# Decay attention and a softplus feed-forward on one core: the middle blocks of the feed-forward at 384 tokens instead of 256, with three output banks and x in four places of 128 tokens

## The chip, the cores and the metric

The kernel runs on one core of a Trainium2 chip. A core has a matrix engine (TensorE, PE), which reads from the on-chip memory SBUF and writes to eight banks of PSUM; a vector engine (VectorE, DVE), a scalar engine (ScalarE, ACT) and a slower general engine (GpSimd, POOL); and a sync engine (SyncE, SP) that issues the DMAs here. Each engine works through its own list of instructions in order, and they wait for each other by semaphores. The metric is the time of one execution on the device, in microseconds (us), less being better. The kernel before takes 1237.31 us, the median of three runs (1235.45 to 1237.55).

## What is computed

Eight batches of 576 tokens, eight heads of 64. First attention with a decay: each score gets the difference of two running sums of log f. Then its output, seen as 4608 tokens of 512 numbers, goes through a feed-forward with 2048 hidden columns and a softplus.

```python
scores = scale * np.matmul(q, k.transpose(0, 1, 3, 2))
log_f = np.log(np.clip(f, 0.0001, 1.0))
cum = np.cumsum(log_f, axis=-1)
decay = cum[:, :, :, None] - cum[:, :, None, :]
scores = np.where(causal, -1000000000.0, scores + decay)
...
x = np.ascontiguousarray(attn_out.transpose(0, 2, 1, 3)).reshape(B * S, H * D)
h = x @ w_in
g = np.maximum(h, 0.0) + np.log1p(np.exp(-np.abs(h)))
return (g @ w_out).astype(np.float32)
```

Inputs are fp32, the two weights 64-bit floats.

## The kernel before

**Numbers in two parts.** Most products are made of rounded numbers (type fp32r) in a high and a low part: an up product takes x high by w high, x low by w high, x high by w low. That is 12 matmuls for each group of 128 hidden columns (`fc`, 16 of them) and a block of tokens: four chunks of 512/128 by three. Down products take the same three pairings of g and w_out, three matmuls of 512 columns for each `fc` and tile of 128 tokens. The high part of w_in (`wih`) and both parts of w_out (`woh`, `wol`) stay in SBUF; the low part of w_in is stored to HBM once (`wil_d`) and loaded again for every block, 512 KB for each two `fc` (`wl`).

**Weights.** The 64-bit weights come in 32 pieces (`load_f64`). A piece is built as fp32 from the two halves of each number by a `scale` (ACT), `clip` (POOL or DVE), `shift`, `low` and `sign` (DVE). Afterwards `split_w_in` and `split_w_out` part it into high and low.

**Attention.** It is cut into 68 jobs: 4 for two heads of the first 256 tokens of batch 0, 8 for the rest of batch 0 by head, then 56, one for each head of batches 1 to 7. Jobs 0 to 11 use plain fp32 matmuls (L723, L853); from job 12 on they are in two parts. A job's score tiles (`s`, L725 and L726) are read by DVE for the row minimum (L730) and by ACT for the exponential (L750); the weights are scaled, turned by PE (`b`, L805), copied by ACT or DVE in two parts (L205, L820), multiplied with v (`o`, L859), and put into the batch's x (`x32`, L877 and L886). Every `s`, `b` and `o` takes one PSUM bank with the tag `att`, of which there are four.

**Feed-forward.** `BLOCKS` cuts the 4608 tokens into 14 blocks of 256 and 2 of 512. Block 0 is plain fp32 (L996, L1100). For the others `split_x` makes the two parts of x, xh and xl, in an array of two halves of 256 tokens: blocks of 256 take turns in the halves (tags x0 and x1), a block of 512 takes both. `up_part` issues six up matmuls (L1016) into a bank `h` (two of them), `gate` computes the softplus of 512 columns of a bank (ACT L1052, L1055, L1058; DVE L1066; high and low parts, L205 and L1074), and `down_part` multiplies with w_out (L1107) into one bank for each tile of 128 tokens: two banks `acc` for a block of 256; a block of 512 takes two more of `att`. The down products of a bank come two banks (`LAG`) after its up products.

**What sets the order.** The program is first written down as operations (`Plan.add`) with what they come after and which buffers (`takes`, `give`) they need. `Plan.run` then puts them in order with an estimate of each one's time: of the next 600 that are free to go it takes the one that could start first. Where it sees PE idle ahead of the first feed-forward output it puts filler matmuls (L1219). A block may be written down once its batch's attention is done (`ready_at`: by job 11, 19, 27 and so on). Feed-forward work is laid between the pieces of the jobs by a share:

```python
until = min((at for at in ready_at if at >= n), default=n)
share = sum(c for c, _ in ffn) / (until - n + 1 + DELAY) / max(1, len(units))
```

So what is at hand is spread over the jobs until the next blocks may begin, and `DELAY` jobs more.

Of the kernel before, what the change touches and what calls it, by code (L numbers as in the profile page):

```python
# [26 lines left out]
DELAY = 6  # L27
# [140 lines left out]
def on_dve(n, fast=False, port=False, bias=0.0):  # L168
    return On("DVE", 0.071 + n / (1920 if fast else 960), bias, fast or port)
# [18 lines left out]
def copies(n):  # L188

    return [on_act(n), on_dve(n, True, bias=COPY_BIAS)]  # L190
# [18 lines left out]
def tile_decay_attention_softplus_ffn(  # L209
# [36 lines left out]
    BUFS = dict(T=2, att=4, h=2, acc=2, xs=1, fe=4, ph=3, pl=3, ph64=2, pl64=2, gh=LAG + 1, gl=LAG + 1, xh=1, xl=1,  # L246
                x32=2, wl=2, vhl=3, vraw=2, raw=1)
    plan = Plan(BUFS | dict(T0=4, stat=4, p=2, x0=1, x1=1, x2=1))
# [147 lines left out]
    def load_f64(src, new, name, takes=()):  # L396
# [27 lines left out]

        def shift(e):
            x = box["x"] = new().bitcast(U32)
            e.tensor_scalar(x, box["t"].bitcast(U32), 3, None, ALU.logical_shift_left)
# [5 lines left out]
        def sign(e):  # L433
            x, h = box["x"], box["t"].bitcast(U32)
            e.scalar_tensor_tensor(x, h, 0x80000000, x, ALU.bitwise_and, ALU.bitwise_or)

# [493 lines left out]
    def ffn_block(i):  # L930

        t0, nt = BLOCKS[i]
        wide = nt > TB
        ntile = nt // P
        nk = 512 // nt
        tags = ("acc", "acc", "att", "att")[:ntile]
        st = {"ups": [], "downs": []}
        plain = i == 0
        half = i % 2
        xtags = ("x0", "x1", "x2") if wide or i == 1 else (f"x{half}",)  # L940

        def split_x():
            if plain:
                st["split"] = [d for a, _, d in wrote[0] if a < TB]
                return
            ready, at = [], t0
            while at < t0 + nt:
                b, o = at // S, at - t0
                lo = at - b * S
                w = min(t0 + nt - at, S - lo, TB - o % TB)  # L950

                def part(x, o=o, w=w):
                    return x_now[x][:, o // TB if wide else half, :, o % TB : o % TB + w]

                def hi_part(e, b=b, lo=lo, w=w, o=o, part=part):
                    if o == 0 and (wide or i == 1):
                        for x in ("xh", "xl"):
                            x_now[x] = buf(x, [P, 2, NCC, TB], f"{x}{i}", F32R)
                    copy(e, part("xh"), x_of[b][:, :, lo : lo + w])

                def lo_part(e, b=b, lo=lo, w=w, part=part):
                    hi = part("xh").bitcast(F32)
                    e.tensor_sub(part("xl"), x_of[b][:, :, lo : lo + w], hi)

                need = [d for a, z, d in wrote[b] if a < lo + w and z > lo]
                h_ = add(
                    copies(NCC * w), hi_part, after=need + ready[:1], takes=() if o else xtags,
                )
                if i == 1 and not o:
                    give("x0", [h_])  # L970
                    give("x2", [h_])
                l_ = add(subs(NCC * w), lo_part, after=[h_])
                ready += [h_, l_]
                splits.setdefault(b, []).append(l_)
                if lo + w == S:
                    give("x32", splits[b])
                at += w
            st["split"] = ready

        def up_part(u, k, part):  # L980
# [8 lines left out]
            def mm(e):  # L989
                if first:  # L990
                    st["h", u] = bank("h", f"h{i}_{u}")
                    st["x", "h"], st["x", "l"] = x_now.get("xh"), x_now.get("xl")
# [8 lines left out]
                if wide:  # L1001
                    o = o.rearrange("p (a t) -> p a t", a=2)
                wl, todo = st["wl", fp], []

                def x(t, cc):
                    t = st["x", t]
                    return t[:, :, cc] if wide else t[:, half, cc]
# [24 lines left out]
            if plain:  # L1032
                for p in pieces:
                    w_in_read.setdefault(p, []).append(op)
                if fc == NFC - 1:
                    splits.setdefault(0, []).append(op)
            elif fc % 2 == 1 and part == 1:
                give("wl", [op])
                if fc == NFC - 1:
                    for x in xtags if i > 1 else ("x1",):  # L1040
                        give(x, [op])

        def gate(fp):
# [3 lines left out]
            def view(a):  # L1047
                return a.rearrange("p (k t) -> p k t", k=nk)
# [132 lines left out]
    for i, (t0, nt) in enumerate(BLOCKS):  # L1181
# [40 lines left out]
    old = nothing  # L1222
    for n in range(len(jobs) + 1):
# [33 lines left out]
        share = sum(c for c, _ in ffn) / (until - n + 1 + DELAY) / max(1, len(units))  # L1257
# [53 lines left out]
```

## Time and profile before

| what | before |
|---|---|
| median of three runs | 1237.31 us (1235.45 to 1237.55) |
| the profiled execution: its own time, its span | 1236.16 us, 1234.4 us |
| mean granted clock of TensorE | 0.994 of full |
| instructions | 21512 |
| moved by DMA | 143.33 MB, mean 116 GB/s |

The profile is of one execution. Its page gives each engine's busy time, groups of equal instructions with their mean time and the idle time ahead of them, and the chain of work that ended last, followed back from the end. In the chain PE has 74% of the span and DVE 13%; L1016 has 28% and L1107 27%. Between two cuts, a table of windows gives each engine's busy time. Times of attention's jobs are those of their first score matmul in the trace: job 12 at 137.1 us, job 24 at 277.2, job 67 at 984.0; the last attention matmul is at 1007.8, and from there PE has the feed-forward alone.

### The profile page before, as it was taken

How to read it: one execution, taken by the hardware profiler on the slowest of the kernel's cores; microseconds unless marked ns; L12 is line 12 of the kernel's file. 1: busy time of each engine (PE TensorE's matmuls, PEld its weight loads, DVE VectorE, ACT ScalarE, POOL GpSimd, SP SyncE). 2: the span in 40 equal slices, each digit the busy share in tenths (PEclk: the TensorE clock that was granted, in tenths of full speed). 3: DMA queues.
4: the chain of work that ended last, by engine and by line, in shares of the span. 5: the costliest groups of instructions: out<-in, count | busy, mean ns of one | idle time of the engine just before them, and what ended most of it. 6: DMA issues, size and time to landing. Idle time of an engine off the chain costs nothing.

```text
span 1234.4 us, 21512 instructions
## 1 busy us (share of the span) xinstructions
PE 1214.8 (98%) x7648; PEld 1066.9 (86%) x7648; DVE 869.1 (70%) x2175; ACT 870.4 (71%) x2069; POOL 156.5 (13%) x130
## 2 busy tenths in 40 slices
PE   8899999999999999999999999999999999999998
PEld 6666678898999999999999999999988999888887
DVE  7898999998887887676777677777778852323322
ACT  5577788978887777676776778677878754444543
POOL 4742011110110111010111001100010100000000
PEclk9899999999999999999999999999999999999999
DMA  7864534443354334343433444334434223211210
GB/s 223 262 176 133 153 92 145 128 123 119 110 152 116 121 109 117 112 130 111 118 119 95 135 118 136 99 114 118 136 102 134 73 69 103 68 52 51 86 52 35
DMA packets 53355, 143.33 MB, mean 116 GB/s; under 512 B 6656, under 2 KB 21016, under 8 KB 53248
## 3 DMA queue, kind: packets, MB, share of 16 engines
q1 hardware_dynamic: 53248, 141.95, 38.5%
q8 instruction: 61, 1.00, 0.4%
q14 instruction: 46, 0.38, 0.1%
HBM read 127.85 MB, written 14.07 MB: 115 GB/s over the span
## 4 chain that ended last, share of the span: by engine, by line
PE 74%; DVE 13%; ACT 5%; DMA 3%; issue 2%; POOL 1%; SPq 1%; DVEq 0%; ACTq 0%; POOLq 0%
PE h L1016 28%; PE acc L1107 27%; PE o L859 6%; PE b L805 6%; PE s L725 3%; PE s L726 3%; DVE s L730 2%; ACT p L773 2%; ACT p L750 1%; DMA raw<-in_qkT 1%; DVE pl L820 1%; PE acc L1100 1%; POOL ti L423 1%; DVE T L681 1%; DMA xl_st<-in_w_out 1%
## 5 line engine op out<-in xcount | busy, mean ns | idle before, releaser
L1016 PE MATMUL h<-xh,wih 128*128 128x256 f32 (+1 forms) x960 | 277.2, 312 | 0.8 <-DVE gl L1074 0.8
L1016 PE MATMUL h<-xl,wih 128*128 128x256 f32 (+1 forms) x960 | 262.9, 297 | 0.0
L1107 PE MATMUL acc<-woh_dt_float32r,gh 128*128 128x512 f32 x544 | 221.8, 408 | 0.0
L750 ACT ACTIVATE p<-s,negm 128x288 f32<-128x288 f32 (+7 forms) x384 | 183.0, 479 | 50.2 <-DVE negm L730 47.7
L1107 PE MATMUL acc<-woh_dt_float32r,gl 128*128 128x512 f32 x544 | 213.4, 392 | 0.0
L1107 PE MATMUL acc<-wol_dt_float32r,gh 128*128 128x512 f32 x544 | 213.0, 391 | 0.0
L1066 DVE SCALAR_TENSOR_TENSOR h<-h,e 128x512 f32<-128x512 f32 x136 | 95.2, 701 | 152.4 <-ACT e L1058 151.9
L775 POOL TENSOR_SCALAR p<-p,rsum 128x448 f32<-128x448 f32 (+4 forms) x77 | 97.7, 1275 | 754.7 <-DVE rsum L764 476.3
L1016 PEld LDWEIGHTS h<-xh,wih 128*128 128x128 f32 x960 | 182.7, 190 | 7.3 <-DVE gl L1074 1.2
L1016 PEld LDWEIGHTS h<-xl,wih 128*128 128x128 f32 x960 | 183.0, 191 | 5.8
L730 DVE CUSTOM_DVE_ANT_0 s<-s,cmask 128x288 f32<-128x288 f32 (+5 forms) x320 | 137.2, 438 | 54.7 <-PE s L726 46.6
L1016 PE MATMUL h<-xh,wl 128*128 128x256 f32 (+1 forms) x960 | 167.9, 297 | 0.0
L1052 ACT ACTIVATE e<-h 128x512 f32<-128x512 f32 x144 | 85.7, 595 | 111.5 <-PE h L1016 109.6
L820 DVE TENSOR_TENSOR pl<-b,ph 128x512 fp32r<-128x512 f32 (+1 forms) x224 | 125.9, 569 | 41.7 <-ACT ph L205 39.5
L805 PE MATMUL b<-ident,p 128*128 128x128 f32 x960 | 147.0, 277 | 7.9 <-ACT p L773 4.2
L1016 PEld LDWEIGHTS h<-xh,wl 128*128 128x128 f32 x960 | 138.4, 190 | 4.9
L805 PEld LDWEIGHTS b<-ident,p 128*128 128x128 f32 x960 | 112.7, 141 | 27.6 <-ACT p L773 6.5
L773 ACT ACTIVATE p<-p,rsum 128x576 f32<-128x576 f32 (+7 forms) x221 | 105.8, 542 | 28.8 <-DVE rsum L764 28.6
L1107 PEld LDWEIGHTS acc<-woh_dt_float32r,gl 128*128 128x128 f32 x544 | 102.2, 188 | 22.7
L1074 DVE TENSOR_TENSOR gl<-h,gh 128x512 fp32r<-128x512 f32 x136 | 93.6, 688 | 34.8 <-ACT gh L205 33.4
L1107 PEld LDWEIGHTS acc<-wol_dt_float32r,gh 128*128 128x128 f32 x544 | 102.9, 189 | 15.0
L1107 PEld LDWEIGHTS acc<-woh_dt_float32r,gh 128*128 128x128 f32 x544 | 102.8, 189 | 15.0
(107 smaller groups left out, 2142.8 us busy)
## 6 DMA issues: line engine op xcount, KB each, us to landing
wl<-wil_d SPq DMA_DIRECT2D x120, 512.0 KB
raw<-in_qkT SPq DMA_DIRECT2D x112, 288.0 KB
vr<-in_vR SPq DMA_DIRECT2D x64, 160.0 KB
out<-ob SPq DMA_DIRECT2D x36, 256.0 KB
sto<-in_w_out SPq DMA_DIRECT2D x11, 512.0 KB
sti<-in_w_in SPq DMA_DIRECT2D x9, 512.0 KB
wil_d<-wil SPq DMA_DIRECT2D x16, 256.0 KB
xh_st<-in_w_in SPq DMA_DIRECT2D x5, 512.0 KB
```

Of the source, the lines that this page charges most:

```text
L730: e.tensor_tensor_reduce(out=box["o"], in0=box["o"], in1=cmask[0:n_q, right - w : right], scale=-0.125, scalar=m0 if i else 3.0e38, op0=AL ...
L750: e.activation(o, box["o"], AF.Exp, bias=m1, scale=-1.0, accum_out=acc)
L773: e.activation(a, a, AF.Copy, scale=f_)
L775: e.tensor_scalar(a, a, f_, None, ALU.mult)
L805: e.transpose(box["ps"][:, at : at + P], pt[pi][:, c : c + P], ident)
L820: e.tensor_sub(box["l"], box["ps"][:, pad : pad + w], box["h"].bitcast(F32))
L859: e.matmul(box["ps"][:, a - g0 : z - g0], st["vhl"][:, vc, :], pbox[x][:, o : o + z - a], start=i == 0 and m == 0, stop=i == len(todo) - 1 ...
L1016: e.matmul(o, l, r, start=m == 0, stop=m == 11)
L1052: e.activation(box["e"], view(st["h", fp]), AF.Abs)
L1066: e.scalar_tensor_tensor(h, h, 0.0, box["e"], ALU.max, ALU.add)
L1074: e.tensor_sub(box["l"], box["t"], box["h"].bitcast(F32))
L1107: e.matmul(st["acc"][tt], l, r[fc], start=fc == 0 and m == 0, stop=fc == NFC - 1 and m == 2,)
```

## The change

Tokens 512 to 3583 are cut into eight blocks of 384 in place of twelve of 256. The array of x has four places of 128 tokens (tags s0 to s3): a block of 384 takes places 0 to 2 or 1 to 3 in turn, so that one place of the next block is free before the block ahead of it is done with the other three; `split_x` works by place, the free one first. A block of 384 has one `fc` in a bank `h` (`nk` is 1), and its gate covers 384 columns. There are three banks `acc` and three `att`; a block of 512 takes three `acc` and one `att`. In `load_f64` the sign is taken as the product of the clipped number and 0.0, on POOL or DVE, into a buffer `gh`, and put in by the shift. `DELAY` is 1, and the share is held below one that spreads what is at hand and what is still to come over all jobs left.

```diff
-DELAY = 6
+DELAY = 1
...
-    TB, WIDE = 256, 512
-    BLOCKS = [(t, TB) for t in range(0, NT - 2 * WIDE, TB)] + [(NT - 2 * WIDE, WIDE), (NT - WIDE, WIDE)]
+    TB = 256
+    BLOCKS = [(0, TB, 0), (TB, TB, 0)]
+    BLOCKS += [(t, 384, t // 384 % 2) for t in range(512, NT - 1024, 384)]
+    BLOCKS += [(NT - 1024, 512, 0), (NT - 512, 512, 0)]
...
-    BUFS = dict(T=2, att=4, h=2, acc=2, xs=1, fe=4, ph=3, pl=3, ph64=2, pl64=2, gh=LAG + 1, gl=LAG + 1, xh=1, xl=1,
+    BUFS = dict(T=2, att=3, h=2, acc=3, xs=1, fe=4, ph=3, pl=3, ph64=2, pl64=2, gh=LAG + 1, gl=LAG + 1, xh=1, xl=1,
...
+        def sign(e):
+            box["z"] = buf("gh", [P, 512], f"z{name}", F32R).bitcast(F32)
+            e.tensor_scalar(box["z"], box["t"], 0.0, None, ALU.mult)
         def shift(e):
             x = box["x"] = new().bitcast(U32)
-            e.tensor_scalar(x, box["t"].bitcast(U32), 3, None, ALU.logical_shift_left)
+            t, z = box["t"].bitcast(U32), box["z"].bitcast(U32)
+            e.scalar_tensor_tensor(x, t, 3, z, ALU.logical_shift_left, ALU.bitwise_or)
...
-        bt = add(on_dve(512, True), shift, after=[bt], takes=takes)
+        bt = add(on, sign, after=[bt], takes=("gh",))
+        bt = add(on_dve(512, port=True), shift, after=[bt], takes=takes)
+        give("fe", [bt])
+        give("gh", [bt])
         bt = add(on_dve(512, port=True), low, after=[bt])
         give(tag, [bt])
-        bt = add(on_dve(512, port=True), sign, after=[bt])
-        give("fe", [bt])
...
-        tags = ("acc", "acc", "att", "att")[:ntile]
+        tags = ("acc", "acc", "acc", "att")[:ntile]
+        st = {"ups": [], "downs": [], "before": range(0)}
+        if i:
+            _, n_, s_ = BLOCKS[i - 1]
+            st["before"] = range(s_, s_ + n_ // P)
+        slots = range(s0, s0 + ntile)
...
+            order = sorted(range(ntile), key=lambda m: (m + s0) in st["before"])
+            for m in order:
...
+                    takes = () if o else (f"s{slot}",)
...
+    def to_come():
+        us = lambda nt: NFC * (2 * on_pe(nt, 6).cost + on_pe(DM, 3 * nt // P).cost)
+        return sum(us(BLOCKS[i][1]) for at, i_s in ready_at.items() if at < len(jobs) - 1 for i in i_s)
...
-        share = sum(c for c, _ in ffn) / (until - n + 1 + DELAY) / max(1, len(units))
+        backlog = sum(c for c, _ in ffn)
+        share = min(backlog / (until - n + 1 + DELAY), (backlog + to_come()) / (len(jobs) - n + DELAY))
+        share /= max(1, len(units))
```

Two places in the order of the instructions. The first is on PE at the first score matmul of job 24 (`s24_0`; the number behind `h` is the block, the next the group of its up products). Before:

```order
L725 MATMUL s24_0_0_3188<-T0_1117 64x64
L726 MATMUL s24_0_0_3188<-T0_1117 64x64
L1016 MATMUL h2_1_3164<-xh1_1486,wih_96 128x256
L1016 MATMUL h2_1_3164<-xl1_1487,wih_96 128x256
L1016 MATMUL h2_1_3164<-xh1_1486,wl2_1_2977 128x256 x4
```

Now:

```order
L1026 MATMUL h2_6_3363<-xl1_1534,wih_96 128x384
L731 MATMUL s24_0_0_3377<-T0_1183 64x64
L732 MATMUL s24_0_0_3377<-T0_1183 64x64
L1026 MATMUL h2_6_3363<-xh1_1533,wih_96 128x384
L1026 MATMUL h2_6_3363<-xl1_1534,wih_96 128x384
```

At the same job block 2 was in its second group of 256 tokens and is now in its seventh of 384. Ahead of this row stood 222 up matmuls of 256 and 84 down matmuls in two parts; now 192 of 256, 78 of 384 and 132 down. At job 12 (`s12_0`) 44 plain up and 12 plain down products of block 0 stood ahead, now 60 and 20. Behind the last attention matmul fewer are left than before.

The second place is DVE where block 6 gets its x. Before (`h4_7` is block 4's last group; its up products are done, and block 5's half was filled long ago):

```order
L205 CAST xh1_1486<-x32_2_2805 128x4x192
L963 TENSOR_TENSOR xl1_1487<-x32_2_2805,xh1_1486 128x4x192
L205 CAST xh1_1486<-x32_3_4227 128x4x64
L963 TENSOR_TENSOR xl1_1487<-x32_3_4227,xh1_1486 128x4x64
L205 CAST ph36_2_5835<-b36_2_5821 128x512
L1066 SCALAR_TENSOR_TENSOR h4_7_5762<-h4_7_5762,e4_7_5816 128x512
```

Now (block 5's group 14 of 0 to 15 is in its gate, `gl5_14`):

```order
L1084 TENSOR_TENSOR gl5_14_7737<-h5_14_7657,gh5_14_7732 128x384
L205 CAST xh1_1533<-x32_3_4403 128x512
L736 ISA s46_1_0_7747,negm2_76<-s46_1_0_7747,cmask_73 128x192
L736 ISA negm2_76 128x1
L975 TENSOR_TENSOR xl1_1534<-x32_3_4403,xh1_1533 128x512 x2
```

and on PE, between block 5's last up product and block 6's first (the last four of nine down matmuls, then two score tiles):

```order
L1117 MATMUL acc5_1_6809<-woh13_dt_float32r_1856,gl5_13_7677 128x512
L1117 MATMUL acc5_2_6810<-woh13_dt_float32r_1856,gh5_13_7664 128x512
L1117 MATMUL acc5_2_6810<-wol13_dt_float32r_1882,gh5_13_7664 128x512
L1117 MATMUL acc5_2_6810<-woh13_dt_float32r_1856,gl5_13_7677 128x512
L731 MATMUL s46_2_0_7771<-T0_1183 128x320
L732 MATMUL s46_2_0_7771<-T0_1183 128x320
L1026 MATMUL h6_0_7777<-xh1_1533,wih_96 128x384
L1026 MATMUL h6_0_7777<-xl1_1534,wih_96 128x384
```

A block's x was split about a block ahead; now two of its three tiles are split between the last up product of the block before and its own first. Seven borders are of this kind; at an eighth, ahead of the first block of 512, three of four places wait.

More of the change, by code (lines that the diff above doesn't have):

```diff
@@ L945, in split_x @@
                 return
[L946 to L975, printed above, removed]
@@ L976, in split_x @@
+            for b in splits:
+                if b * S + S in range(t0 + 1, t0 + nt + 1):
                     give("x32", splits[b])
-                at += w
             st["split"] = ready
@@ L1000, in mm @@
                     return
-                if wide:
-                    o = o.rearrange("p (a t) -> p a t", a=2)
+                o = o.rearrange("p (a t) -> p a t", t=P)
                 wl, todo = st["wl", fp], []
                 def x(t, cc):
-                    t = st["x", t]
-                    return t[:, :, cc] if wide else t[:, half, cc]
+                    return x_now[f"x{t}"][:, s0 : s0 + ntile, cc]
                 for cc in range(NCC):
@@ L1039, in up_part @@
                 if fc == NFC - 1:
-                    for x in xtags if i > 1 else ("x1",):
-                        give(x, [op])
+                    for slot in slots:
+                        give(f"s{slot}", [op])
         def gate(fp):
@@ L1180, in tile_decay_attention_softplus_ffn @@
     ready_at = {}
-    for i, (t0, nt) in enumerate(BLOCKS):
+    for i, (t0, nt, _) in enumerate(BLOCKS):
         last = t0 + nt - 1
```

41 lines of the change are left out of this document (30 added, 11 removed).

## The prediction

> **What bounds the kernel now.** I read the engine totals first, then a table by stretches of time, then the chain that ended last. The totals say that TensorE (PE) is busy nearly throughout, and that no other engine is:
>
> ```profile
> PE 1214.8 (98%) x7648; PEld 1066.9 (86%) x7648; DVE 869.1 (70%) x2175; ACT 870.4 (71%) x2069; POOL 156.5 (13%) x130
> ```
>
> An average over stages can deceive, so here are the stages. The rows give the stretch in us, its length, then busy time and instructions of PE, PE's weight loads, DVE, ACT and POOL, the granted clock, DMA share and GB/s. The cuts are near the first score matmul of jobs 5, 12, 24 and 60 and the end of attention.
>
> ```profile
> 0.00:59.00 59.00, 50.73 (x279) 39.16 (x279) 47.47 (x124) 31.77 (x81) 36.14 (x40) 0.91 0.80 243
> 59.00:137.00 78.00, 76.77 (x347) 49.63 (x347) 71.45 (x187) 58.45 (x142) 22.62 (x14) 1.00 0.55 167
> 137.00:277.00 140.00, 137.71 (x894) 116.76 (x893) 132.69 (x364) 119.47 (x311) 20.16 (x18) 1.00 0.43 121
> 277.00:880.00 603.00, 601.14 (x4186) 557.54 (x4185) 452.32 (x1147) 458.99 (x1117) 66.09 (x50) 1.00 0.41 119
> 880.00:1004.00 124.00, 121.97 (x854) 112.30 (x853) 96.54 (x257) 97.40 (x248) 11.46 (x9) 1.00 0.33 100
> 1004.00:1234.00 230.00, 226.50 (x1098) 191.49 (x1096) 68.64 (x100) 104.33 (x172) 0.00 (x0) 1.00 0.19 65
> ```
>
> From 277 us on PE is the bound: DVE and ACT have 25% free (452 and 459 of 603), and the clock is whole. From 137 to 277 us DVE (132.7 of 140) and PE are both full; before that weights are converted, and part of PE's time is filler:
>
> ```profile
> L1219 PE MATMUL fill<-cmask 128*128 128x128 f32 x194 | 28.4, 300 | 2.3 <-POOL cmask L296 2.3
> ```
>
> A PE that is "busy" need not be at its peak, since ends of matmuls are modelled. So I price matmuls by their pace in the chain of waits, late in the run, where nothing else holds PE (start, length, what; the last of the five rows is from the mixed stretch):
>
> ```profile
> 1008.89 2.75 PE acc L1107 x12
> 1011.64 2.87 PE h L1016 x24
> 1053.70 5.44 PE h L1016 x24
> ...
> 186.28 1.72 PE acc L1100 x4
> ```
>
> An up matmul of 256 tokens takes 2.87/24 = 0.1196 us, one of 512 tokens 5.44/24 = 0.2267, a down matmul 2.75/12 = 0.229, a plain fp32 down record 1.72/4 = 0.43 (a plain up record is half as wide: 0.215, an estimate).
>
> How full is PE really? The next rows are the same table for single lines (columns: stretch, length, PE busy, weight loads busy): L1016 in two stretches, L1107 in the same two, L996, L1100, and L726 in two.
>
> ```profile
> 137.00:277.00 140.00, 32.78 (x222) 29.09 (x222) 1.00 0.43 121
> 277.00:880.00 603.00, 255.29 (x1770) 228.22 (x1770) 1.00 0.41 119
> ...
> 137.00:277.00 140.00, 21.91 (x84) 14.96 (x84) 1.00 0.43 121
> 277.00:880.00 603.00, 231.56 (x877) 156.19 (x878) 1.00 0.41 119
> ...
> 137.00:277.00 140.00, 10.67 (x43) 6.98 (x41) 1.00 0.43 121
> ...
> 137.00:277.00 140.00, 18.86 (x40) 7.07 (x40) 1.00 0.43 121
> ...
> 137.00:277.00 140.00, 21.08 (x72) 13.09 (x72) 1.00 0.43 121
> 277.00:880.00 603.00, 62.59 (x214) 38.87 (x214) 1.00 0.41 119
> ```
>
> L726 runs six times in a job, so 137 to 277 us holds 72/6 = 12 jobs (11.7 us each) and 277 to 880 us 35.7 (16.9 each). In the latter the feed-forward takes 1770 x 0.1196 + 878 x 0.229 = 412.8 us; what is left of 603, 190.2, is 5.33 us of attention per job. With that, 137 to 277 us asks PE for 26.5 + 19.2 + 9.2 + 17.2 + 12 x 5.33 = 136.2 us of its 140. **PE has hardly any idle time after 59 us**: 3.8 us there, and 78 - 76.77 plus 2.3 of filler before, 7.3 in all. A gain must come from less PE work, or from those few us.
>
> **The change, part by part.**
>
> *Wider up products.* 3072 tokens in twelve blocks of 256 (12 x 192 = 2304 matmuls) become eight blocks of 384 (8 x 192 = 1536). Before: 2304 x 0.1196 = 275.6 us. A matmul of 384 is not in the trace; on the straight line through 0.1196 and 0.2267 it takes 0.1731 us (12.5 ns a matmul plus 0.418 ns a token): 265.9. That is **-9.6 us**. Bounds from the nearest rows: at 256's price per token 0 us, at 512's (0.170 us each) -14.4. I take the line, since 384 lies midway. Nothing hides it, as PE is the bound. The Trainium skill (TensorE: Matmul & The Clock Gate, "Back-to-back issue gap") gives N/2.4 + 2.5 ns for a warm matmul. By its 2.5 ns the 768 matmuls fewer would save 1.9 us and the sum below would be 1239.4; the trace's 12.5 ns disagrees, and the measurement decides.
>
> *Gates, copies and loads off the path.* 96 gates of 512 columns become 128 of 384: more fixed cost on ACT and DVE, hidden in 277 to 880 us by their free 25%. Loads of the low half of w_in fall from 120 to 88, beside a DMA share of 0.41:
>
> ```profile
> wl<-wil_d SPq DMA_DIRECT2D x120, 512.0 KB
> ```
>
> Both count 0. Where that cover is missing, while DVE is full, only one of the wide blocks begins (in job 21).
>
> *Weights.* The sign step moves from DVE's last place to a product by 0.0 on POOL or DVE. Shift becomes one of the 0.68 us kind and the sign's "or" goes:
>
> ```profile
> L427 DVE TENSOR_SCALAR wol_dt_float<-to 128x512 uint32<-128x512 uint32 x15 | 7.8, 527 | 2.2 <-POOL to L423 2.2
> L435 DVE SCALAR_TENSOR_TENSOR woh_dt_float<-ti,woh_dt_float 128x512 uint32<-128x512 uint32 x16 | 10.9, 685 | 0.1
> L423 POOL TENSOR_SCALAR to<-to 128x512 f32<-128x512 f32 x12 | 24.4, 2043 | 23.9 <-ACT to L420 15.2 <-DVE negm L730 4.8 <-DVE x L205 2.4
> ```
>
> DVE loses 32 of about 0.49 us and gains 26 such (16 signs, 10 clips moved from POOL): about -3 us. POOL goes from 22 to 28 at 2.04: +12 us, and a piece whose clip and sign both run there comes 2 us later. I take 0, between -3 and +4.
>
> *Work moved forward.* DELAY falls from 6 to 1. By the order above, at job 24's first score matmul 192 up matmuls of 256, 78 of 384 and 132 down matmuls have been issued, against 222, 0 and 84: 66.7 us against 45.8. These 20.9 us no longer stand later, but they enter a stretch with 7.3 us to spare. Gain between 0 and -7.3; I take **-3**, as DVE is full there too.
>
> *A hole after block 1.* Sooner done, block 1 leaves PE alone with attention until batch 1 is finished and block 2 may start: 138 rows lie between them, 36 down matmuls (8.2 us) and about 9.7 us of attention, 1.8 jobs. Those take 1.8 x 11.7 = 21.3 us at the pace seen, against 17.9: 0 to +3.4, I take **+2**.
>
> *Splits of x at a block's border.* Before, half of the x buffer was free, and a block was split a block ahead. Now one of three places is free and two wait for the last up product of the block before. The nearest case stands ahead of the first block of 512, on DVE:
>
> ```profile
> 1048.27 0.70 DVE L205 CAST xh<-x 128x1024 fp32r<-128x1024 f32 x1 [1.61 <-PE h L1016]
> 1049.00 1.23 DVE L963 TENSOR_TENSOR xl<-x,xh 128x1024 fp32r<-128x1024 f32 x1
> ```
>
> Two places are 1024 columns: 1.96 us from the first start, plus a row minimum of about 0.5 that stands between. The cover by the order is nine down matmuls (2.06) and two score pairs (0.5). So 0 to 1 us at each of eight borders; I take **+2**, range 0 to +8. Queued behind a late split are PE's up products, in order, and so attention's.
>
> *Three banks for attention instead of four.* This is the cost that the trace doesn't show. The holds are seen near 200 us, one bank each for transposes, scores and output:
>
> ```profile
> 200.28 0.77 PE L805 MATMUL b<-ident,p 128*128 128x128 f32 x5
> 202.37 0.68 DVE L820 TENSOR_TENSOR pl<-b,ph 128x512 fp32r<-128x512 f32 x1
> ...
> 200.80 0.38 PE L725 MATMUL s<-T 128*128 128x288 f32 x1
> 203.97 0.19 ACT L750 ACTIVATION_READ_ACCUMULATOR p<-s,negm 128x1 f32 x1
> ...
> 202.13 0.38 PE L859 MATMUL o<-ph,vhl 128*128 128x256 f32 x1
> 205.33 0.38 DVE L886 TENSOR_TENSOR x<-o,x 64x256 f32<-64x256 f32 x1
> ```
>
> That is 2.8, 3.4 and 3.6 us. A job has 6 score, 4 transpose and 2 output banks: 20.4 + 11.2 + 7.2 = 38.8 bank-us, 9.7 us on four banks, **12.9 us on three**. From 277 us on a job takes 16.9 us and this is covered. Jobs 12 to 23 are not: PE will be asked for 12 x 5.33 + 66.7 + 12.0 (rest of block 0) = 142.7 us, 11.9 a job. Bounds: 0 (part of a hold is waiting in DVE's queue, which a later score matmul spares) and 12 x (12.9 - 11.9) = +12. I take **+3**. The Trainium skill (Perfetto Trace Analysis, "Optimization Strategy") says that the same gap repeating on the engine that should be full can mean too little PSUM for the next tile. This trace shows little of it so far, 9.4 us in the whole run (engine, line, what it waited for, us, times, longest):
>
> ```profile
> PEld s L725 <- ACT p L750: 6.2, 13, 1.5
> ...
> PE s L725 <- ACT p L750: 3.2, 3, 1.4
> ```
>
> *Sum.* The profiled execution spans 1234.4 us, 2.9 below the median of the runs, 1237.3. 1234.4 - 9.6 - 3 + 2 + 2 + 3 = 1228.8; with 2.9 added, **1231.7 us**.
>
> **The rivals.**
>
> *All cover holds.* No new wait, the idle 7.3 us is used, the line holds: 1237.3 - 9.6 - 7.3 = 1220.4; with 512's price 1215.6. For it: PE's order is planned, and the mid stretch shows nearly no gap. Against: DVE full to 277 us.
>
> *Given back.* The wider matmul saves its 9.6, but the hole, the borders and the banks take 9 to 10 in place of 7, and the work moved forward gains nothing: 1235 to 1240, near 1237. That is also where a change would land that leaves the bound as it is; the order shows that it does what it says.
>
> *The banks decide: slower.* In jobs 12 to 23 the pace becomes that of three banks. The other terms leave -8.6, so it turns slower once the stretch costs over 11 us more, at 12.8 us a job or a mean hold of 3.2 us, just what is seen now (38.8/12 = 3.23). At a hold of 3.4 a job takes 13.6 us, 163 against 142.7: +20.5, so 1249. Against: holds are shorter where DVE isn't full.
>
> *All cost is in the tokens.* Fewer matmuls then save nothing: 1237.3 - 3 + 2 + 2 + 3 = 1241.3. Against: 0.1196/256 is 0.467 ns a token, 0.2267/512 is 0.443. The skill's page named above comes near to this rival.
>
> **How the numbers follow.** A measurement can tell about 0.2% (2.5 us) from no change. Forecast, 1222 to 1234.8: 0.44; all cover holds, below 1222: 0.14; given back, within 2.5 us of 1237.3: 0.20; above 1239.8: 0.22, of it 0.19 for the banks and 0.03 for all cost in the tokens. So faster 0.58, same 0.20, slower 0.22. The range leaves out a tenth on each side: below 1217 is more than the bounds of matmul and idle time give together but for 1.4 us, and above 1247 the holds would have to lengthen.
>
> **What would show it.** Right: up products of 384 at 0.173 us in the chain; attention's end at a later us but a shorter tail; job 24 later than 277 us by some 10 to 16 us, with block 2 seven groups into its ups. Wrong: 384 at 0.179 or 0.163; gaps ahead of score matmuls released by ACT L750 or by the x additions (the banks); gaps ahead of a block's first up product released by DVE's subtraction (the borders); a slower first 59 us (the conversions).

## The result, and the profile after

The changed kernel takes **1247.83 us** (median of five runs, 1246.05 to 1250.15) where the kernel before, run beside it on the same chip, takes 1236.03 (1235.45 to 1237.55). The ratio is 1.0094, 95% interval 1.0082 to 1.0106: slower by about 11.7 us, where 5.6 us faster was forecast, and just above the upper end of the forecast's range (1247 us). The profiled spans say the same, 1246.0 us against 1234.4.

The totals of the changed kernel's page, in the form of those of before:

```profile
PE 1213.8 (97%) x6854; PEld 1054.6 (85%) x6854; DVE 892.5 (72%) x2283; ACT 881.2 (71%) x2172; POOL 155.8 (13%) x141
```

PE is busy for as long as before (1214.8), though it has less to do. So the stages again: stretch, length, busy time and instructions of PE, its weight loads, DVE, ACT and POOL, granted clock, DMA share, GB/s. The cuts are near the first score matmul of jobs 5, 12, 24 and 60 and the end of attention, now at later times:

```profile
0.00:61.00 61.00, 49.22 (x276) 37.25 (x277) 49.18 (x120) 35.32 (x91) 37.59 (x42) 0.97 0.76 220
61.00:151.00 90.00, 88.45 (x377) 56.44 (x376) 79.34 (x195) 63.74 (x149) 26.94 (x17) 1.00 0.55 169
151.00:308.00 157.00, 149.39 (x937) 128.86 (x937) 134.05 (x365) 127.31 (x333) 16.54 (x14) 0.98 0.39 110
308.00:925.00 617.00, 610.04 (x3640) 557.50 (x3640) 469.65 (x1248) 464.58 (x1188) 57.58 (x54) 1.00 0.33 96
925.00:1046.00 121.00, 120.55 (x738) 110.76 (x738) 96.79 (x258) 96.88 (x254) 15.72 (x14) 1.00 0.29 83
1046.00:1246.00 200.00, 196.15 (x894) 163.80 (x892) 63.51 (x103) 93.35 (x162) 1.41 (x1) 1.00 0.17 57
```

The tail is 30 us shorter (200 for 230): work did move forward. But jobs 12 to 23 take 157 us for 140, PE idles 7.6 of them (before 2.3), and the clock is no longer whole. Jobs 24 to 59 idle 7.0 us (before 1.9).

To see where time is lost and not only moved, I compare the start of each job's first score matmul with before, and take off the feed-forward work that was issued ahead of it beyond what was issued before, priced by the paces of the prediction. Job 24 starts at 308.5 us for 277.2, 31.3 later, with 20.9 us more feed-forward work ahead of it: 10.4 us are lost. I call this the loss; at the end it is what the execution is longer, plus the 9.7 us of feed-forward work saved at these prices. It is read from one execution of each kernel. Three executions whose order on PE is the same up to job 19 (the changed kernel and two with fillers, below) have -0.3, -2.1 and -2.2 us at job 12, so a single figure is good to some 2 us; from job 12 to 18 they lose 2.9, 2.5 and 2.5, so a stretch is told better.

| loss, us, up to | job 12 | 16 | 20 | 22 | 24 | 26 | 54 | 60 | end |
|---|---|---|---|---|---|---|---|---|---|
| changed kernel | -0.3 | -0.7 | 2.0 | 9.8 | 10.4 | 7.9 | 17.5 | 22.5 | 21.3 |

Three places stand out: jobs 20 to 22, a slow leak from 26 to 54, and jobs 54 to 60.

**Jobs 20 to 22, the hole.** Block 1's matmuls are issued by 255.6 us, and block 2's first up product comes at 268.0. The timeline of PE's matmuls, where it sat idle (start, length, what; in brackets the idle time and what ended it):

```profile
258.01 1.10 PE L811 MATMUL b<-ident,p 128*128 128x128 f32 x6 [1.41 <-ACT p L756]
...
264.70 0.35 PE L865 MATMUL o<-ph,vhl 128*128 128x256 f32 x1 [0.99 <-DVE pl L826]
...
267.61 0.41 PE L731 MATMUL s<-T 128*128 128x320 f32 x1 [0.73 <-DVE x L892]
...
268.67 0.63 PE L1026 MATMUL h<-xl,wih 128*128 128x384 f32 x1 [0.33 <-DVE xl L975]
```

Attention alone cannot keep PE busy here: it waits for the exponential, for the low part of attention's weights, for an output bank and, at block 2's first up products, for the split of x. The table of windows shows a second thing, in the third column from the end:

```profile
256.50:258.00 1.50, 0.10 (x1) 0.00 (x0) 0.84 (x6) 1.47 (x5) 1.15 (x1) 1.00 0.98 289
258.50:262.00 3.50, 3.50 (x16) 2.94 (x14) 2.12 (x6) 2.03 (x6) 0.00 (x0) 0.51 0.22 44
262.00:268.50 6.50, 4.25 (x27) 3.29 (x26) 5.87 (x20) 5.94 (x18) 1.21 (x2) 1.00 0.01 4
268.50:272.00 3.50, 3.33 (x13) 3.24 (x14) 2.80 (x7) 2.28 (x8) 0.61 (x1) 0.54 0.16 47
```

After each cluster of gaps the granted clock is half for about 3.4 us. PE counts as busy there, but its matmuls take twice as long (transposes start 0.11 us apart at 258.2 us, 0.21 at 260). Before the change there was one such place past 60 us, after a gap at job 24. The prediction's "the clock is whole" passes over it: in its row of 603 us a dip of 3.4 us is rounded away. The gap and the dip:

```profile
278.00:279.50 1.50, 0.30 (x4) 0.10 (x2) 1.25 (x5) 1.24 (x4) 0.00 (x0) 1.00 0.00 0
280.50:284.00 3.50, 3.50 (x18) 3.41 (x17) 2.94 (x10) 2.85 (x10) 1.40 (x1) 0.51 0.18 47
```

**Jobs 54 to 60, a pause of attention.** The chain that ended last, from 800 us on (start, length, what):

```profile
801.28 1.09 PE o L865 x10
...
819.19 2.09 PE acc L1117 x9
821.28 0.66 PE o L865 x6
...
826.19 2.10 PE h L1026 x12
828.29 2.08 PE acc L1117 x9
...
847.12 2.12 PE h L1026 x12
...
850.22 0.39 DVE x L892
...
851.55 0.33 DVE x L892
```

The outputs of job 52 and of half of job 53 (`o`, the first written at 795.2, then at 801.1 and 821.1 us) are put into x only at 850.2 to 853 us. They hold all three banks of attention, for 55, 51 and 32 us. They wait for a buffer of `x32`: of two, one holds batch 4 until block 8's first tile (tokens 2816 to 2943) is split, and by its turn of places that tile goes where block 7 still is; block 8's early place takes its third tile. PE loses nothing at once, as it has feed-forward work (h and acc in turn), but that work is then missing beside the jobs that follow. This reading is tested below.

### The profile page after: what moved, and what is told of

The parts are those of the page before. It is cut to its first block, busy times and chain, and to the rows that moved or that the text cites. A ratio compares the mean times of both kernels' runs of the same rounds, so it can differ in the third digit from the quotient of the medians.

```text
span 1246.0 us, 20217 instructions
## 1 busy us (share of the span) xinstructions
PE 1213.8 (97%) x6854; PEld 1054.6 (85%) x6854; DVE 892.5 (72%) x2283; ACT 881.2 (71%) x2172; POOL 155.8 (13%) x141
## 4 chain that ended last, share of the span: by engine, by line
PE 59%; DVE 21%; ACT 12%; issue 4%; DMA 3%; POOL 0%; DVEq 0%; SPq 0%; POOLq 0%; ACTq 0%
PE h L1026 20%; PE acc L1117 20%; PE b L811 6%; ACT p L756 4%; PE o L865 4%; DVE s L736 3%; DVE pl L826 2%; PE s L731 2%; DVE h L1076 2%; PE acc L1110 2%; PE s L732 2%; ACT p L779 2%; DVE T L693 2%; DMA raw<-in_qkT 1%; DMA sti<-in_w_in 1%
## 5 line engine op out<-in xcount | busy, mean ns | idle before, releaser
L1026 PE MATMUL h<-xh,wih 128*128 128x384 f32 (+2 forms) x704 | 251.1, 359 | 0.7 <-DVE gl L1084 0.7
L1026 PE MATMUL h<-xl,wih 128*128 128x384 f32 (+2 forms) x704 | 239.4, 343 | 0.5 <-DVE xl L975 0.3
L1076 DVE SCALAR_TENSOR_TENSOR h<-h,e 128x384 f32<-128x384 f32 (+1 forms) x168 | 99.9, 595 | 179.0 <-ACT e L1068 178.3
L781 POOL TENSOR_SCALAR p<-p,rsum 64x64 f32<-64x64 f32 (+3 forms) x83 | 91.2, 1107 | 809.1 <-DVE rsum L770 461.7
L1062 ACT ACTIVATE e<-h 128x384 f32<-128x384 f32 (+1 forms) x176 | 90.8, 516 | 106.1 <-PE h L1026 105.3
L1026 PE MATMUL h<-xh,wl 128*128 128x384 f32 (+2 forms) x704 | 154.6, 341 | 0.0
L811 PEld LDWEIGHTS b<-ident,p 128*128 128x128 f32 x960 | 112.8, 142 | 36.4 <-ACT p L756 10.7
L1026 PEld LDWEIGHTS h<-xl,wih 128*128 128x128 f32 x704 | 133.4, 189 | 6.8 <-DVE xl L975 1.0
L826 DVE TENSOR_TENSOR pl<-b,ph 128x64 fp32r<-128x64 f32 (+1 forms) x224 | 124.5, 570 | 16.0 <-ACT ph L205 13.4
L1084 DVE TENSOR_TENSOR gl<-h,gh 128x384 fp32r<-128x384 f32 (+1 forms) x168 | 98.5, 586 | 48.2 <-ACT gh L205 47.1
L205 ACT CAST gh<-h 128x384 fp32r<-128x384 f32 (+1 forms) x141 | 71.8, 509 | 83.4 <-DVE h L1076 82.5
```

Of the source, the lines that this page charges most:

```text
L205: (e.tensor_copy if hasattr(e, "tensor_copy") else e.copy)(out, in_)
L781: e.tensor_scalar(a, a, f_, None, ALU.mult)
L811: e.transpose(box["ps"][:, at : at + P], pt[pi][:, c : c + P], ident)
L826: e.tensor_sub(box["l"], box["ps"][:, pad : pad + w], box["h"].bitcast(F32))
L1026: e.matmul(o, l, r, start=m == 0, stop=m == 11)
L1062: e.activation(box["e"], view(st["h", fp]), AF.Abs)
```

## Experiments: the banks, the share, the weights

Every kernel below computes the whole result. Ratios are to the kernel before on the same chip.

**Three banks alone, in the kernel before.**

```diff
-    BUFS = dict(T=2, att=4, h=2, acc=2, ...
+    BUFS = dict(T=2, att=3, h=2, acc=2, ...
```

> The kernel before with three banks for attention's scores, transposes and outputs instead of four (one PSUM bank stays unused); all else as before. Theory of the banks: most of the 21 us that the changed kernel lost on TensorE come from the fourth bank, so this one alone costs 10 to 18 us: 1247 to 1255 us, with gaps ahead of score matmuls in the middle stretch. Theory of the share: the loss comes from block 1 being done too soon and the hole behind it; then this one is within 4 us of before: 1236 to 1240.

1247.65 us, ratio 1.0102 (1.0079 to 1.0124): one bank fewer costs what the whole change costs. The loss is 0.3 us at job 12, 8.5 at job 20, 8.9 at 24 and 12.0 at 54. Jobs 12 to 23 of this kernel in one window, and two windows around one of its waits:

```profile
137.00:288.00 151.00, 144.63 (x911) 122.66 (x910) 132.22 (x348) 124.81 (x314) 16.90 (x15) 0.97 0.39 112
...
212.40:214.00 1.60, 0.00 (x0) 0.01 (x1) 1.42 (x3) 1.31 (x3) 0.00 (x0) 1.00 0.42 147
216.50:226.70 10.20, 7.98 (x31) 6.59 (x31) 8.84 (x26) 5.91 (x19) 1.40 (x1) 0.51 0.29 77
```

The wait itself, on the timeline of PE's matmuls:

```profile
214.02 0.37 PE L725 MATMUL s<-T 128*128 128x288 f32 x1 [1.65 <-DVE pl L820]
```

A score matmul waits 1.65 us for the bank that DVE's subtraction L820 gives back, more gaps follow, and the clock is half for 10 us. Most of the loss is made there, in jobs 16 to 20.

**DELAY and share alone, in the kernel before** (`DELAY = 1` and the two lines of the share as in the change).

> The kernel before with DELAY 1 and the new share (blocks of 256 and four banks for attention as before). Theory of the share: the hole behind block 1 costs about 8 us here too: 1243 to 1246 us. Theory of the banks: with four banks attention keeps its pace in the hole, so 0 to 3 us: 1236 to 1239.

1238.39 us, 1.0029 (1.0017 to 1.0041). The work moved forward gains nothing: 2.9 us are lost at job 12, 8.1 at 20, 3.7 at the end. In its jobs 12 to 23 PE idles 5.2 us, with four banks, for 2.3 before.

**The old share in the changed kernel.**

```diff
-DELAY = 1
+DELAY = 6
-        share = min(backlog / (until - n + 1 + DELAY), (backlog + to_come()) / (len(jobs) - n + DELAY))
+        share = backlog / (until - n + 1 + DELAY)
```

> The changed kernel with the old share and DELAY 6 (blocks of 384 and three banks for attention stay). Theory of the share: the 8 us of the hole come back: 1239 to 1241 us. Theory of the banks: the stretch is paced by the banks whatever the share, so 0 to 4 us come back: 1244 to 1248.

1250.44 us, 1.0128 (1.0111 to 1.0145): neither theory had it slower. The loss is 12.7 us at job 24, and attention pauses twice, at job 44 (banks held 52, 43 and 26 us) and at job 52 (77, 70 and 51).

**The weights' steps**, old ones in the changed kernel, and new ones alone in the kernel before.

> The changed kernel with the weights built as before (clip, shift, low, sign). Both theories: the first 59 us were only 2 us later, and by 97 us nothing was lost, so within 2 us of the changed kernel, 1246 to 1250 us. A rival, that the moved sign step delays the start, expects 1244 or less.

> The kernel before with the new steps of the weights alone (sign as a product by 0.0 on POOL or DVE, put in by the shift). The changed kernel with the old steps was 2.5 us slower than with the new. If the steps are worth the same by themselves: 1232-1234 us, ratio 0.997-0.999, gained before job 12. If they were worth it only beside the other changes: 1234.5-1237 us, ratio 0.999-1.002. The prediction took 0, between -3 and +4.

With the old steps the changed kernel takes 1250.29 us, 1.0125 (1.011 to 1.014), just above what was expected: 2.5 us more by the times, 3.8 by the ratios. Alone the new steps give 1235.34 us, 0.9998 (0.9989 to 1.0007): nothing. The trace shows why: 6.4 us are gained by job 12, and from job 18 to 22, where attention waits for its own engines, they are given back (gain 5.9 us at job 18, loss 2.0 at 22).

**Four banks in the changed kernel.**

```diff
-    BUFS = dict(T=2, att=3, h=2, acc=3, ...
+    BUFS = dict(T=2, att=4, h=2, acc=2, ...
-        tags = ("acc", "acc", "acc", "att")[:ntile]
+        tags = ("acc", "acc", "att", "att")[:ntile]
```

> The changed kernel with four banks under attention's tag and two under the outputs' (as before); a block of 384 takes its third output bank from attention, so attention has four banks until block 2's down products begin (job 22) and three after. Theory of the banks: of the 10.4 us lost up to job 24 some 6 to 10 come back: 1238 to 1242 us. If the loss there is the share's (block 1 done too soon): 1246 to 1250.

1254.46 us, 1.0152 (1.0135 to 1.017), a miss. The early part is as expected, the loss at job 24 is 2.2 us in place of 10.4. But a wide block now takes one of the four for its third tile, the pause at job 52 stays, and from job 54 to 60 another 16.2 us go, with the clock at half for 10.2 us there. This way the banks could not be told from the rest.

**The planner's lag.** In the stretch of the slow leak (365 to 800 us) this row leads the waits of PE's weight loads (total us, times, longest):

```profile
PEld s L731 <- DVE x L892: 3.2, 10, 0.6
```

A small wait, again and again, for an output bank. The Trainium skill (Perfetto Trace Analysis, "Optimization Strategy") says that the same gap, repeating on the engine that should be full, can mean too little SBUF or PSUM for the next tile. This trace agrees, with ten waits, 3.2 us in all. I planned a bank's release later:

```diff
-PELAG, GLAG, PORTLAG = 0.1, 0.2, 0.09
+PELAG, GLAG, PORTLAG = 0.1, 0.6, 0.09
```

> The changed kernel with the planner's lag for a bank given back raised from 0.2 to 0.6 us, so that score matmuls are planned later behind the release of their bank. If the middle stretch (jobs 30 to 54, 7.7 us lost) loses by score matmuls that stand in PE's order just where their bank comes free, that loss falls by 3 us or more and the time is 1242-1245 us. If it loses for another reason: 1246-1250 us.

1248.67 us, 1.0106 (1.0091 to 1.0121). From job 30 to 54 the loss is 1.2 us in place of 7.7, and between 400 and 800 us the row above shrinks from 2.9 us in nine waits to 0.3 in one. That speaks for scores that stand in the order right at a bank's release, though the lag changes the whole order. The time is that of the other expectation: 19.7 us are lost by job 30, in place of 9.8, with the clock at half for 17.1 us from 253 us on and for 6.8 from 383 (half of these is 12.0 us; in the changed kernel it is 3.4). The lag moves the loss and does not remove it.

## Experiments: the wide blocks, the pause, and a faster version

**Every second block's tiles turned round**, so that the free place takes the tile that ends a batch.

```diff
+        turn = s0 == 1
+        def place_of(m):
+            return ntile - 1 - m if turn else m
...
-                    slot = s0 + m
+                    slot = s0 + place_of(m)
```

> The changed kernel with the three tiles of every second block of 384 in turned order, so that the free place always takes the block's first tile, which holds the end of a batch. Theory: attention's outputs of job 52 no longer hold all three banks for 55 us waiting for a batch's x to come free, and the some 4 us lost in jobs 54 to 60 come back: 1243 to 1245 us. Rival: TensorE had feed-forward work throughout that pause, so nothing changes: 1246 to 1250.

1243.77 us, 1.0062 (1.0042 to 1.0081). The pause at job 52 is gone, 17.9 us are lost at job 60 for 22.5. By the medians the turn is worth about 4 us; 2.8 of them lie in jobs 54 to 60, where 2.1 us are lost for 4.9, so the pause cost 3 to 4. A long hold does not cost by itself: at job 60 of this kernel outputs hold their banks for 31 and 21 us, and no loss follows.

**All blocks of 256, everything else as changed.**

```diff
-    BLOCKS += [(t, 384, t // 384 % 2) for t in range(512, NT - 1024, 384)]
+    BLOCKS += [(t, TB, t // TB % 2 * 2 ^ 2) for t in range(512, NT - 1024, TB)]
```

> The changed kernel with blocks of 256 in place of 384 (three output banks of which two are used, three banks for attention, new share, new weights). It measures what the width is worth with all else equal. If wide blocks only save their 9.6 us on TensorE: 1255 to 1259 us. If in the middle and late stretches they lose about as much again (late splits, the pause in attention, outputs that hold banks): 1244 to 1249.

1240.44 us, 1.0037 (1.0024 to 1.005), below both expectations. The profiled execution, the fastest of ten (1237.38), loses 1.2 us by its end; no output of attention holds its bank over 5 us, and the clock is whole from 60 to 1234 us. By the median, three banks, the share and the new weights' steps cost 4.6 us together, where in the kernel before the bank alone cost 12.6 and the share alone 3.6: these costs do not add. The blocks of 384 save 6.8 us of matmuls (at 0.175 us each, see below), and yet with them the kernel is 7 us slower: beside their matmuls they cost some 14.

**256 up to token 1279, then six blocks of 384**, the tiles turned as above, and banks four and two, or three and three.

```diff
-    BLOCKS += [(t, 384, t // 384 % 2) for t in range(512, NT - 1024, 384)]
+    BLOCKS += [(t, TB, 2 - t // TB % 2 * 2) for t in range(512, 1280, TB)]
+    BLOCKS += [(t, 384, (t - 1280) // 384 % 2) for t in range(1280, NT - 1024, 384)]
```

> Blocks of 256 up to token 1279 and of 384 from there, attention with four banks until the first wide block (about job 33), first tile in the free place, new share and weights. If the banks in jobs 16 to 30 and the pause at job 52 are what was lost: 1230 to 1235 us, under both kernels. If something else in the wide blocks costs: 1238 or more.

> As the version with 256 tokens up to 1279 and 384 behind (1231.43 us, ratio 0.9972), but with three banks for attention and three for outputs. If attention's banks are what was lost, most of it between jobs 12 and 24: 1236-1242 us, the loss there 5 us or more over the four-bank version's (which lost 5.3 us between jobs 12 and 24 after a start 4.9 us ahead). If the width of the early blocks alone was it: 1230-1234 us, a loss by job 24 within 2 us of the four-bank version's.

With four banks it takes **1231.43 us**, 0.9972 (0.9959 to 0.9984), faster than both kernels. Its windows, cut at jobs 12, 24 and 60 and at the end of attention (the fourth stretch, 904 to 1032, is left out):

```profile
146.00:304.00 158.00, 152.17 (x1019) 132.63 (x1018) 140.34 (x382) 125.83 (x327) 22.66 (x19) 1.00 0.39 116
304.00:904.00 600.00, 597.37 (x3738) 549.62 (x3737) 467.16 (x1228) 459.38 (x1164) 60.75 (x54) 1.00 0.35 103
...
1032.00:1228.00 196.00, 192.59 (x873) 160.28 (x871) 60.53 (x97) 93.21 (x163) 1.09 (x1) 1.00 0.16 58
```

PE still idles 5.8 us in jobs 12 to 23, but with no dip of the clock, and the middle idles 2.6 us where the changed kernel idles 7.0. With three banks it takes 1237.97 us, 1.0019 (1.0009 to 1.0028). Only the banks differ: 0.47%, 5.8 us. By the profiled runs, which are further apart than the medians, 3.9 are lost before job 12 and 3.1 from job 12 to 24, where 5 or more were expected. Of all kernels without fillers, from job 16 to 26, the four with four banks lose -0.1 to 6.6 us (the share alone 1.9, the weights alone 6.6, four banks in the changed kernel 2.2, four with 256 in front -0.1), the eight with three banks 2.5 (all blocks of 256) to 12.1 (the lag), with medians of 2.0 and 8.3. So the bank counts there, though any new order may lose some. And from the changed kernel with turned tiles (1.0062) to this one (1.0019) only the first 768 tokens behind block 1 differ, in two blocks or in three, and with them which places the later blocks take: 0.43%, 5.3 us.

**Fillers in the hole.** Does the lower clock cost time, where DVE and ACT are nearly full? Nine filler matmuls go ahead of two waits of the hole (shown for the first; four more stand ahead of `o19_1`); first written to the bank that is waited for, then to a free output bank.

```diff
+                if f"{n}_{bi}" == "19_0":
+                    filling.append(bank("acc", "fill2"))
+                    for _ in range(5):
+                        e.matmul(filling[-1][:, 0:P], cmask[:, 0:P], cmask[:, 0:P], start=True, stop=True)
                 box["ps"] = bank("att", f"b{n}_{bi}")
```

> The changed kernel with nine filler matmuls (128x128, plain fp32, no part of the result) in two waits of the hole behind block 1: five ahead of job 19's first transposes (a gap of 1.41 us), four ahead of its second output (a gap of 0.99 us). In the changed kernel the granted clock is half from 258.6 to 262 us and from 268.6 to 272 us, 3.4 us lost. If that is lost because PE stood idle just before: a clock of 1.00 between 250 and 280 us, and 2.5-4 us less than the changed kernel (1244-1245.5 us, ratio 1.006-1.0075). If the clock falls for another reason, or costs nothing since DVE and ACT set the pace there: within 1 us of the changed kernel or slower by the fillers (1247-1249 us).

> The same nine fillers in the version with 256 tokens up to 1279 and three banks (1237.97 us, ratio 1.0019), where the clock was half for 10 us, 5.1 us lost. If the gaps set the clock and the clock the time: 1232.5-1235 us, ratio 0.9975-0.9995. If not: 1237-1239.5 us.

> As with the nine fillers before, but written into a free output bank, so that they stand in PE's order ahead of the two waits and wait for nothing. (Before, they had been given the waiting banks and ran behind the waits: the gaps of 1.41 and 0.99 us stood, the clock stayed at 1.00 from 60 us on, and the time was 1245.78 us, ratio 1.0084.) If the lower clock is what costs time in the hole: 1244-1245.5 us, ratio 1.006-1.0075, the loss between jobs 20 and 26 smaller by 2.5 us or more (5.9 us in the changed kernel). If the hole is set by DVE and ACT, and PE's clock costs nothing there: ratio 1.008-1.0105, that loss within 1 us of 5.9, the clock 1.00 all the same.

> The same in the version with 256 tokens up to 1279 and three banks (clock half for 10 us there, 5.1 us; 1.0019 without fillers, 1.0023 with fillers behind the waits). If the clock costs time: ratio 0.9975-1.000. If not: 1.001-1.0035.

The first pair gave 1245.78 us (1.0084, 1.0067 to 1.0101) and 1238.48 (1.0023, 1.0014 to 1.0033), no change that can be told. Those fillers ran behind the waits: the gaps stood, the fillers' own 1.4 and 1.1 us came on top, and in both profiled executions the clock stayed whole in the hole all the same. In the second pair they run in the gaps. The changed kernel with them, on its timeline and in a window:

```profile
254.06 1.28 PE L812 MATMUL fill<-cmask 128*128 128x128 f32 x10
...
255.63 0.88 PE L815 MATMUL b<-ident,p 128*128 128x128 f32 x6 [0.30 <-ACT p L756]
```

```profile
256.00:272.00 16.00, 14.15 (x94) 12.13 (x93) 14.00 (x39) 14.05 (x38) 1.81 (x2) 1.00 0.24 59
```

The three-bank version in windows, without fillers (two rows) and with them (one):

```profile
256.00:257.40 1.40, 0.01 (x1) 0.00 (x0) 0.75 (x4) 1.37 (x5) 1.06 (x1) 1.00 1.03 310
258.00:268.70 10.70, 9.72 (x44) 8.80 (x43) 7.47 (x22) 7.06 (x19) 0.34 (x1) 0.52 0.06 14
```

```profile
256.00:272.00 16.00, 15.35 (x116) 13.99 (x117) 14.03 (x40) 14.50 (x39) 1.09 (x1) 1.00 0.34 97
```

The clock stays whole. That the fillers did it, one execution does not show: the kernel with all blocks of 256 has a gap of 1.42 us at the same place (253.5 to 255.0 us) and no fillers, and its clock stays whole too:

```profile
250.00:255.00 5.00, 3.58 (x24) 2.93 (x22) 4.08 (x16) 4.22 (x13) 1.77 (x1) 1.00 0.40 108
255.00:260.00 5.00, 4.46 (x27) 3.21 (x27) 3.50 (x9) 3.70 (x11) 0.00 (x0) 1.00 0.20 43
260.00:265.00 5.00, 4.16 (x34) 4.11 (x35) 4.78 (x19) 4.97 (x13) 1.09 (x1) 1.00 0.02 5
```

All executions together show it for the changed kernel: its mean granted clock is 0.990 to 0.996 in five, and 0.997 to 0.999 in the nine with fillers of either kind.

In the three-bank version the time falls to 1235.42 us, 1.0004 (0.9994 to 1.0013) from 1.0019, about 2 us, though the intervals overlap a little; between jobs 20 and 26 the loss falls from 2.6 to -0.3. The changed kernel comes to 1244.35 us, 1.0086 (1.0068 to 1.0104), which alone is too near to 1.0094 to tell, and lies where the clock was expected to cost nothing; its loss between jobs 20 and 26 falls from 5.9 to 4.0, and with the fillers behind the waits it stayed at 6.0.

The clock's price can also be read without fillers, from executions of one kernel that were granted different clocks. The changed kernel took 1246.05 us at 0.996 and 1250.15 at 0.990: 7.5 us of full clock less, 4.1 us more. Of ten executions of the three-bank version the one at 0.998 took 1236.91 and the two at 0.993 1239.35: 6.2 us less, 2.4 more. So the lower clock costs about half of what it withholds (3.4 and 5.1 us in the hole of the two kernels), some 2 us. Why not all of it, is not shown; in the hole PE also waits for DVE and ACT.

## Why the prediction was wrong, step by step

- **Wider up products, -9.6: right in kind, 2.8 us too much.** Twelve matmuls of 384 stand in the chain with 2.10 us, 0.175 each, for 0.1731 predicted, so 1536 of them save 6.8 us. The bound from 512's price (0.170) and the rival that all cost is in the tokens (0.179) fall. The loss above, at the predicted price, counts the difference as lost: 2.9 of 21.3 us at the end, 1.7 of 9.6 from job 26 to 54.
- **Gates, copies and loads, 0: not separated.** Beside its matmuls the width costs some 14 us in all, the pause at job 52 among them, and how much of it is these was not measured.
- **Weights, 0: right for the whole.** Alone they give 0.9998; beside the rest they save 2.5 to 3.8 us, around the lower end of -3 to +4.
- **Work moved forward, -3: wrong.** The 20.9 us ahead of job 24 are there as the order says, but the share alone costs 0.29%, 3.6 us, in the kernel before. Job 24 came 31.3 us later, not 10 to 16. The idle 7.3 us were not a place where work fits: in jobs 12 to 23 PE idled 2.3 us, mostly in waits of attention, and with the share alone it idled 5.2. That more feed-forward work beside DVE and ACT makes more such waits would explain it; this was only argued.
- **The hole, +2 (0 to 3.4): mis-sized.** Between jobs 20 and 26 5.9 us are lost. The prediction priced it by job pace, with PE at full speed in the hole; behind gaps of 1.41 and 0.99 us the clock was half, worth some 2 us. The gaps themselves are waits for the exponential, for a bank and for a late split, which a mean pace does not show.
- **Splits at the borders, +2: right, or less.** The row of the group on the page shows 0.3 us behind DVE's subtraction, in the whole run (ahead of the weight loads it is 1.0):

```profile
L1026 PE MATMUL h<-xl,wih 128*128 128x384 f32 (+2 forms) x704 | 239.4, 343 | 0.5 <-DVE xl L975 0.3
```

- **Three banks, +3, and beside them the wide blocks' other costs, +4 (hole 2, borders 2, gates 0): the step that failed.** "From 277 us on a job takes 16.9 us and this is covered. Jobs 12 to 23 are not": alone, three banks cost 1.02%, 12.6 us, most of it in jobs 16 to 20; in the step between the two versions with 256 in front 5.8. With all blocks of 256, banks, share and weights together cost 4.6 us, where the prediction's terms for them add up to 0; the width then costs 14 beside its matmuls, in place of 4. So both were undersized, the width by more. Whether they cost more together than apart, no run tells: narrow blocks with four banks, the share and the new steps were not run.
- **Why the mean hold misled.** With three banks the holds by the trace became shorter (in the changed kernel a score's in jobs 12 to 19 3.15 us for 3.43, and 33.1 bank-us in a job for 37.5), so that three banks would allow 11.0 us a job; the pace was 13.1 all the same. What costs are single waits where a release comes late, such as 1.65 us, and the clock behind them: in the kernel before with three banks PE idles 6.4 us in jobs 12 to 23 for 2.3, and the clock is half for 10.2 us. At the half worth found above that makes 6.7 of the 8.6 us lost there, an estimate. "Covered" fell too: from job 26 to 54 the changed kernel loses 9.6 us, 7.7 of them behind job 30, where the longer lag left 1.2. With three banks and blocks of 256 that stretch loses 3.8 us (all blocks narrow) and 5.0 (the kernel before with three banks), so the width has a part in it. 1.7 us are the price of the matmul; which other instructions do the rest stays open.
- **Not in the prediction: the pause at job 52**, 3 to 4 us. The prediction read the borders for PE's sake and not for the buffer that a split frees. More places of x, or a third buffer `x32`, would test it as well; neither was tried.
- **The rivals.** "The banks decide" gave 1249 us, and 1247.8 was measured, but it put 20.5 us into jobs 12 to 23, where 10.7 are lost; the other half lies behind job 24, where it put no cost of the banks. So its number came near by luck. "Given back" had the hole, the borders and the banks at 9 to 10 us and no gain from the work moved forward; all losses together were 18 to 21.

Taken off one by one, starting from the changed kernel, the costs are these: from 1.0094, turned tiles take off 0.32%, narrow blocks up to token 1279 0.43%, a fourth bank for attention 0.47%, which is 0.9972. That is 4.0, 5.3 and 5.8 us by 1236, in this order; in another order the shares would differ, as the run with four banks alone in the changed kernel shows.

## What to carry to other kernels

A bank taken from a pipeline is not priced by mean hold times banks per job: look in the trace for the waits whose release is already the last to come, since a small delay there repeats or opens a gap. Try a wider block first behind the stretch in which another stage sets the pace; here wide blocks behind token 1279 were worth 5.3 us over wide blocks from 512 on. Price parts of a change in the new kernel too: a bank cost 12.6 us in the old one, and the bank, the share and the steps together 4.6 with narrow blocks. When a place in a buffer ring changes, follow what the freed place releases upstream: a split that comes late held an SBUF buffer, this held PSUM banks, and these held attention.

## What was not expected of the hardware

Gaps of PE of 1.0 to 1.65 us, none of them longer, were followed by half the clock, within 3 us of the end of the last of them: for 3.4 us after a single cluster and for 10 us where more gaps followed (the rows above at 258.5, 216.5 and 258.0 us). A gap alone does not decide: behind the gap of 1.42 us in the kernel with all blocks of 256 the clock stayed at 1.00. What decides is not shown. The Trainium skill (TensorE: Matmul & The Clock Gate, "HAM oscillation — how this bites in real kernels") gives as its abstract rule to have no idle gaps of PE beyond about 3.4 us; in these runs gaps of less than half of that were followed by half the clock, and the measurement decides.
